# Seven batches of gates transposed by VectorE and DRAM rows, two rows of running sums for the first two slots, and a new list of steps

## The chip, the cores and the metric

The kernel runs on one core of a Trainium2 chip. The metric is the device time of one execution in microseconds (us), lower is better, as the median of several runs. Besides those runs, one execution was profiled; durations are read from that one.

The engines are called PE (TensorE, the matrix unit; PEld is its weight load), DVE (VectorE), ACT (ScalarE), POOL (GpSimd) and SP (SyncE, which here does nothing but issue transfers, in order).

## The reference

The program is a causal attention with a bias from running sums, followed by a mixture of four attention experts of which each token uses two. Cut to what matters:

```python
B, H, S, D = 8, 8, 576, 64
# attention, for each of 64 heads
scores = q @ k.T / sqrt(D)
cum = cumsum(maximum(s, 0))
scores = where(causal, -1e9, scores + minimum(-(cum[:, None] - cum[None, :]), 0))
attn = softmax(scores) @ v
x = heads_side_by_side(attn)                      # 8 batches x 576 x 512
# experts
logits = x @ w_gate                               # 4 per token
topk, w = two_largest(logits), softmax over the two
for e in range(4):
    q, k, v = x @ wq[e], x @ wk[e], x @ wv[e]
    ye = causal_softmax(q @ k.T / sqrt(64)) @ v @ wo[e]
    out += (gate weight of e, zero where not chosen) * ye
```

## The kernel before, in words

**Slots.** The work is a list of 50 slots, numbered 0 to 49, each for a pair of heads: four slots of attention for each of the eight batches, and between them two slots of experts for the batch before. (Slots -2 and -1 only prepare, slot 49 finishes.) A slot's work is cut into small steps, named by a letter and a number. Those that matter here:

- `ld`, `h0` to `h3`, `l0` to `l3`, `lq`, `lk`: loads q and k of a pair (`raw`) and splits them into a leading part (tiles `q_2`, `k_2` and so on, ring `Q2`, `K2`) and a rest (`Q1`, `K1`), for score products that use both.
- `hc`: puts the running sums as extra rows under the keys, from row 64 on, so that the score product adds the bias.
- `m0` to `m5` and `M0` to `M5`: PE multiplies queries and keys into `mx`, DVE takes each row's maximum (line 752) into `mcol`.
- `mt`, `mA`, `mq`: PE transposes the maxima, ACT negates them into `mr` (line 776), SP issues two transfers (line 781) that write them as row 96 of the queries. The score products need that row.
- `s0` to `s6`, `E0` to `E6`: score products on PE, exponentials on ACT into `p`.
- `b`, `d`: POOL masks the diagonal and adds up the columns into `r`. `v0` to `v8`: PE multiplies `p` and `r` by the values (line 914).
- `p0` to `p7`: projections of the experts (line 1144). `g0` to `g3`: the gates of a batch, into tile `gw` (128 x 5 x 4).
- `t0`, `T0`, `t1`, `T1`, `td`: PE transposes `gw` with five small products (line 1256), ACT copies the result to a row tile (line 1263), and one transfer (`gcol<-g`, line 1268) spreads it over the partitions, where it later scales the reciprocals of the expert slots (line 1000).
- `i0` to `i59`: 60 spare products on a tile of zeros (line 1376) that feed no result and keep PE at work in slot -2.

**Order.** The whole order is one written list, `ORDER`, of entries `slot:step`. Each engine executes its own instructions in the order of that list; an instruction waits on semaphores for its operands and for its buffer. All transfers go through the one SP queue, so a transfer that waits holds back all behind it. PE's results go to eight banks that are handed round in the order of the list.

**Slots 0 and 1** (`DIRECT`) don't split their heads: the tile `plain` holds q and k as loaded, and the score products (line 800) run on it in full precision. The running sums of all heads stand in `early`, part of the buffer `PB[1]` (its tile is `p` in the rows), as three rows that add up to the sum: two splits on DVE (`c3`, `c4`; lines 464 and 467) make the leading part, the next part and the rest. `hc` of slots 0 and 1 takes these three rows straight from there, with four transfers (two heads, 512 and 64 columns each; line 631). All other slots take theirs from DRAM (`cum`).

## Time and profile before

| | us |
|---|---|
| median of three runs | 662.95 |
| lowest, highest run | 659.91, 663.21 |
| the profiled execution, its time | 661.08 |
| span of its trace | 659.4 |
| PE busy in the span | 645.2 |
| DVE, ACT, POOL busy | 508.8, 471.6, 414.9 |
| transfers' engines busy, share of the span | 47% |

The span runs from the first to the last instruction of the trace. Busy time of PE counts a product until its modelled end, and products overlap, so the distance between the starts of two neighbours is what a product takes from the line.

### The profile page before, as it was taken

To read this page: it belongs to the slowest core of one execution; us is meant where nothing else is said; L and a number is where in the kernel's file an instruction comes from. 1 tells how busy PE (TensorE), PEld (TensorE's weight loads), DVE (VectorE), ACT (ScalarE), POOL (GpSimd) and SP (SyncE) were. 2 spreads that over 40 slices of the span, in tenths; PEclk is the share of its full clock that TensorE was granted. 3 is DMA by queue.
4 is the path that set the end of the run, shared out by engine and by line. 5 is a ranking of instruction groups with operands and counts; after the bars stand their busy time and mean duration, and the time that the engine had idled before them with its cause. 6 is when DMAs were issued, how large, how long until landed. Compare 5 with 4: busy or idle time off the path is not lost.

```text
span 659.4 us, 16622 instructions
## 1 busy us (share of the span) xinstructions
PE 645.2 (98%) x5921; PEld 531.6 (81%) x5922; DVE 508.8 (77%) x1452; ACT 471.6 (72%) x1091; POOL 414.9 (63%) x557
## 2 busy tenths in 40 slices
PE   7799999999999999999999999999999999999997
PEld 3377698888887898788888888878888888898875
DVE  6488878887888678885789859887788867771884
ACT  3459978877778667787578867687587877576564
POOL 9179756687576665864687639746966668626130
PEclk9799999999999999999999999999999999999999
DMA  6325544533646355564565444636554634320513
GB/s 169 101 91 129 168 134 103 145 93 92 161 114 153 99 127 137 135 187 117 128 163 145 124 115 120 172 104 165 114 161 109 169 68 120 101 88 21 133 40 112
DMA packets 49165, 81.23 MB, mean 123 GB/s; under 512 B 19494, under 2 KB 19494, under 8 KB 49084
## 3 DMA queue, kind: packets, MB, share of 16 engines
q1 hardware_dynamic: 49084, 80.18, 46.3%
q8 instruction: 47, 0.77, 0.5%
q14 instruction: 34, 0.28, 0.1%
HBM read 44.55 MB, written 10.09 MB: 83 GB/s over the span
## 4 chain that ended last, share of the span: by engine, by line
PE 94%; DVE 2%; ACT 1%; DMA 1%; issue 0%; SPq 0%; DVEq 0%; ACTq 0%
PE pvp L914 20%; PE pq L1144 16%; PE s L806 11%; PE s L811 11%; PE mx L738 10%; PE pw L1144 8%; PE po L1144 7%; PE sm L967 4%; PE s L845 1%; PE s L800 1%; PE po L1118 1%; PE mt L772 1%; PE i L1376 1%; DMA q<-mr 1%; PE gt L1256 1%
## 5 line engine op out<-in xcount | busy, mean ns | idle before, releaser
L752 DVE CUSTOM_DVE_ANT_0 sink<-mx,mask 128x64 bf16<-128x64 f32 (+7 forms) x432 | 168.8, 428 | 70.6 <-PE mx L738 56.0
L827 ACT ACTIVATE p<-s 128x512 f32<-128x512 f32 x288 | 160.8, 591 | 44.3 <-PE s L811 32.8
L857 POOL TENSOR_SCALAR_AFFINE_SELECT p<-p 128x256 f32<-128x256 f32 (+1 forms) x192 | 90.8, 481 | 126.5 <-ACT p L827 103.7
L806 PE MATMUL s<-q,k 128*128 128x192 f32 (+2 forms) x552 | 151.9, 299 | 0.0
L811 PE MATMUL s<-q,k 97*128 97x192 f32 (+2 forms) x552 | 141.6, 291 | 0.7 <-DMA q<-mr 0.6
L878 POOL TENSOR_TENSOR r<-r,p 128x640 f32<-128x640 f32 (+1 forms) x92 | 128.6, 1398 | 4.8
L806 PEld LDWEIGHTS s<-q,k 128*128 128x128 f32 x552 | 105.2, 191 | 10.1 <-issue 3.7
L811 PEld LDWEIGHTS s<-q,k 97*128 97x128 f32 x552 | 105.2, 191 | 1.7 <-DMA q<-mr 1.1
L1144 PE MATMUL pq<-x,wqkh 128*128 128x288 f32 x512 | 105.1, 299 | 0.0
L914 PE MATMUL pvp<-p,v 128*64 128x128 f32 (+3 forms) x1024 | 100.6, 322 | 0.0
L713 DVE TENSOR_TENSOR q<-raw,q 64x576 fp32r<-64x576 f32 x92 | 81.7, 905 | 20.1 <-ACT q L678 14.1
L719 DVE TENSOR_TENSOR k<-raw,k 64x1024 fp32r<-64x1024 f32 (+1 forms) x92 | 80.0, 883 | 18.0 <-PE s L806 8.0
L738 PE MATMUL mx<-k,q 96*64 96x256 bf16 (+7 forms) x920 | 87.1, 293 | 0.0
L1144 PEld LDWEIGHTS pq<-x,wqkh 128*128 128x128 f32 x512 | 81.4, 188 | 1.4 <-issue 0.4
L914 PEld LDWEIGHTS pvp<-p,v 128*64 128x64 f32 x1024 | 63.5, 136 | 21.6 <-issue 2.2
L1144 PE MATMUL pq<-x,wqkl 128*128 128x288 f32 x256 | 75.5, 295 | 0.0
L875 POOL TENSOR_TENSOR r<-p 128x384 f32<-128x384 f32 x46 | 47.8, 1038 | 38.6 <-ACT p L827 35.1
L682 ACT ACTIVATE k<-raw 64x128 fp32r<-64x128 f32 (+1 forms) x92 | 61.4, 680 | 10.1 <-DMA raw<-in_qk_dram 5.8
L678 ACT ACTIVATE q<-raw 64x576 fp32r<-64x576 f32 x92 | 61.5, 678 | 4.8 <-DMA raw<-in_qk_dram 3.1
L738 PEld LDWEIGHTS <-q 96*64 96x64 bf16 x920 | 45.9, 110 | 21.5 <-issue 7.5
L857 POOL TENSOR_SCALAR_AFFINE_SELECT r<-p 128x256 f32<-128x256 f32 x48 | 31.5, 655 | 35.4 <-ACT p L827 35.4
L928 ACT ACTIVATE pv<-pvp 128x256 f32<-128x256 f32 (+1 forms) x92 | 36.3, 407 | 23.3 <-PE pvp L914 23.0
(143 smaller groups left out, 1181.6 us busy)
## 6 DMA issues: line engine op xcount, KB each, us to landing
raw<-in_qk_dram SPq DMA_DIRECT2D x30, 576.0 KB
rb<-rr SPq DMA_DIRECT2D x92, 144.0 KB
q<-q SPq DMA_DIRECT2D x45, 288.0 KB
k<-k SPq DMA_DIRECT2D x39, 288.0 KB
v<-in_vm_dram SPq DMA_DIRECT2D x32, 256.0 KB
out_dram<-o SPq DMA_DIRECT2D x32, 256.0 KB
q<-mr SPq DMA_DIRECT2D x92, 2.2 KB
w_qk<-in_wqk_dram SPq DMA_DIRECT2D x4, 256.0 KB
```

What stands on the lines that cost most here:

```text
L678: nc.scalar.activation(q2[0:64, j], get_raw(n)[0:64, j], AF.Copy)
L713: nc.vector.tensor_tensor(a[64:128, j], get_raw(n)[0:64, j], q2[0:64, j].bitcast(F32), op=OP.subtract)
L719: nc.vector.tensor_tensor(part(c[0:64]), get_raw(n)[64:128, :, k], part(c[64:128]).bitcast(F32), op=OP.subtract)
L738: nc.tensor.matmul(t[64 * j : 64 * j + 64, c0 : c0 + k1 - k0], q2[0:RC, 64 * qt : 64 * qt + 64], keys(n)[0:RC, span(j, k0, k1)].bitcast(BF ...
L752: nc.vector.tensor_tensor_reduce(sink[:, c0 : c0 + w], t[:, c0 : c0 + w], mask[:, m0 : m0 + w], scale=1.0, scalar=mcol[n][:, 9:10] if bi = ...
L806: nc.tensor.matmul(t[0:nk, c0 : c0 + q1 - q0], K1[r1(n)][:, span(j, k0, k0 + nk)], Q1[r1(n)][:, j, q0:q1], start=True, stop=False,)
L811: nc.tensor.matmul(t[0:nk, c0 : c0 + q1 - q0], K2[r2(n)][0 : RM + 1, span(j, k0, k0 + nk)], Q2[r2(n)][0 : RM + 1, j, q0:q1], start=False, ...
L827: nc.scalar.activation(ptile[n][:, x % 2, 512 * ci : 512 * ci + 512], tl[x], AF.Exp, scale=0.125)
L857: nc.gpsimd.affine_select(out=a if kt else running()[:, :, 0:128], in_=a, pattern=[[64 if kt == 4 else 0, 2], [1, nk]], compare_op=OP.is_g ...
L878: add(r[:, :, q0:S], r[:, :, q0:S], p[:, :, 1024 + c : 1024 + c + S - q0], op=OP.add)
L914: nc.tensor.matmul(cur[h][64 * j : 64 * j + 64, q0 - PVC[h] : q1 - PVC[h]], vsl(j, kt), rtile[n][:, j, 0:128] if own else ptile[n][:, j, c ...
L1144: nc.tensor.matmul(t[0:nk, 0:w], l, r, start=(x == 0), stop=(x == len(terms) - 1))
```

## The change

Three edits. First, for seven of the eight batches (all but the last) the five PE transposes of `gw` and their two ACT copies go. In their place `tv` is one DVE transpose of a 128 x 32 tile (`gwt`, of which `gw` now is the first 20 columns) in blocks of 32 x 32, `ts` writes its rows to DRAM with four transfers, and `td` reads them back spread over the partitions. Second, slots 0 and 1 take two rows of running sums, leading part and rest, which the first split alone makes; the tail of their scores is two products of 64 x 64, and queries and keys stand in one tile. Third, `ORDER` is new as a whole (3951 entries for 3967).

```diff
 ORDER = (
-    "-2:i37 -2:i18 -2:i23 -2:i7 -2:i21 -2:i39 -2:i12 -2:i31 -2:f12 -2:i9 -2:i30 -2:i22 -2:f20 "
...
+    "-2:i33 -2:i25 -2:i10 -1:z2 -2:z1 -2:i13 -2:i34 0:ld -2:f12 -2:f22 -2:z2 -2:i9 1:h2 -2:i18 "
...
-    gw = const.tile([P, 5, E], F32, tag="gw", name="gw")
+    gwt = const.tile([P, 32], F32, tag="gw", name="gw")
+    gw = gwt[:, 0 : 5 * E].rearrange("p (t e) -> p t e", e=E)
...
-        def split(j):
-            c = t["c"][:n]
+        def cut(x, y):
             nc.vector.tensor_single_scalar(
-                c3[:n, j].bitcast(I32), c.bitcast(I32), -65536, op=OP.bitwise_and
+                y[:n].bitcast(I32), x[:n].bitcast(I32), -65536, op=OP.bitwise_and
             )
-            nc.vector.tensor_tensor(c3[:n, 2] if j else c, c, c3[:n, j], op=OP.subtract)
...
+        def first():
+            cut(t["c"], c4[:, 1])
+            nc.vector.tensor_tensor(c4[:n, 0], t["c"][:n], c4[:n, 1], op=OP.subtract)
+
+        def second():
+            cut(c4[:, 0], c4[:, 2])
+            nc.vector.tensor_tensor(c4[:n, 3], c4[:n, 0], c4[:n, 2], op=OP.subtract)
...
         def sums_in():
             for j in range(2):
                 hd = 2 * i + j
-                for k in (slice(0, 512), slice(512, S)):
-                    nc.sync.dma_start(
-                        keys(n)[64:67, span(j, k.start, k.stop)], early[0][hd : hd + 1, :, k]
-                    )
...
+                nc.sync.dma_start(whole(n)[64:66, 2 + j], early[0][hd : hd + 1, 0:2])
...
             if n in DIRECT:
-                nc.tensor.matmul(
-                    t[:, 0:P], keys(n)[:, 0:P], queries(n)[:, :, q], start=True, stop=True
-                )
+                for j in range(2):
+                    h = slice(64 * j, 64 * j + 64)
+                    nc.tensor.matmul(
+                        t[h, h], keys(n, P, j, 512, S), queries(n)[:, j, q], start=True, stop=True
+                    )
                 return
...
+        def flip():
+            t["w"] = sb.tile([P, 32], F32, tag="gwt", name=f"gwt{b}", bufs=1)
+            nc.vector.transpose(t["w"], gwt)
+
+        def out_rows():
+            t["d"] = dram.tile([E, S], F32, tag="gd", name=f"gd{b}", bufs=2)
+            for x in range(4):
+                m = 5 if x < 2 else 4
+                d = t["d"].rearrange("e (c i) -> c e i", i=32)[x : x + 4 * m - 3 : 4]
+                nc.sync.dma_start(d, t["w"][32 * x : 32 * x + E * m])
+
         def send():
             gcol[b] = sb.tile([P, S // 32], F32, tag="gcol", name=f"gcol{b}", bufs=2)
-            nc.sync.dma_start(gcol[b], t["g4"])
+            nc.sync.dma_start(gcol[b], t["d"].rearrange("e (p c) -> (e p) c", c=S // 32))
...
         if b < B - 1:
-            items["td"] = send
+            items["tv"], items["ts"], items["td"] = flip, out_rows, send
         else:
+            items["t0"], items["T0"] = lambda: turn(0), lambda: copy(0)
+            items["t1"], items["T1"] = lambda: turn(1), lambda: copy(1)
             items["sl"] = select
```

The order of instructions changes in many places; three of them follow. The first is ACT at the start of the program. Before, its first operand to wait for is the sums' input (`s_t`):

```order
L452 ACT_TABLE_LOAD
L452 ACTIVATE s_r<-s_t 64x576
L678 ACTIVATE q_2_70<-raw_155 64x576
L706 ACTIVATE k_0_66<-raw_155 64x1024
L706 ACTIVATE k_0_66<-raw_155 64x128
```

Of the changed kernel, the same place:

```order
L670 ACT_TABLE_LOAD
L670 ACTIVATE q_0_68<-raw_120 64x576
L452 ACTIVATE s_r<-s_t 64x576
L670 ACTIVATE q_0_68<-raw_120 64x576
L698 ACTIVATE k_1_67<-raw_120 64x1024
```

A copy from a pair's loaded heads (`raw_120`, here those of slot 3) now stands ahead of the sums' input. In the SP queue that pair's load moved to the front as well. Before, the queue opens so (`p_94` is the buffer with the running sums):

```order
L448 DMA s_t<-in_s_dram 64x576
L563 DMA raw_155<-in_qk_dram 128x2x576
L643 DMA plain<-in_qk_dram 64x2x576
L495 DMA w_qk_177<-in_wqk_dram 128x512
L637 DMA plain<-in_qk_dram 64x2x64
L637 DMA plain<-in_qk_dram 64x2x512 x2
L631 DMA plain<-p_94 3x1x512
L631 DMA plain<-p_94 3x1x64
```

And in the changed kernel:

```order
L566 DMA raw_120<-in_qk_dram 128x2x576
L448 DMA s_t<-in_s_dram 64x576
L636 DMA plain<-in_qk_dram 64x2x576
L635 DMA plain<-in_qk_dram 64x2x576 x2
L566 DMA raw_215<-in_qk_dram 128x2x576
L632 DMA plain<-p_94 2x1x576 x2
L636 DMA plain<-in_qk_dram 64x2x576
L632 DMA plain<-p_94 2x1x576 x2
```

Two transfers instead of four bring the sums of a slot, and a second pair's load stands ahead of them. The second place is PE after the maxima of slot 0 (`mt_289`, `mt_330` are the transposes of slot 0's maxima, `i` spare products, `s_4` and so on the score chunks of slot 0). Before, with the rows between left out:

```order
L738 MATMUL mx_3_282<-plain 64x512
L772 MATMUL mt_289<-ident,mcol_251 9x128
L738 LDWEIGHTS plain
L738 MATMUL mx_3_301<-plain 64x512
...
L1376 MATMUL i_306<-sink 128x512
...
L738 MATMUL mx_5_335<-plain 64x256
...
L1376 MATMUL i_387<-sink 128x512
L800 MATMUL s_4_389<-plain 128x320
L800 MATMUL s_4_389<-plain 128x192
L1376 LDWEIGHTS sink
L1376 MATMUL i_392<-sink 128x512
```

Of the changed kernel:

```order
L730 MATMUL mx_4_326<-plain 64x512
L764 MATMUL mt_330<-ident,mcol_282 9x128
L1381 LDWEIGHTS sink
L1381 MATMUL i_332<-sink 128x512
...
L1381 MATMUL i_389<-sink 128x512
L792 MATMUL s_5_392<-plain 128x320
L792 MATMUL s_5_392<-plain 128x192
L792 MATMUL s_4_397<-plain 128x320
L792 MATMUL s_4_397<-plain 128x192
L792 MATMUL s_0_403<-plain 128x256
L792 MATMUL s_0_403<-plain 128x256
```

All six `mx` banks of slot 1 moved ahead of `mt`, the spare products after `mt` stand in one run of 20 (before, 11 and then 9 more among products of slots 0 and 1), and the six score chunks follow each other with none between. The third place is the gates of the first batch. PE before:

```order
L806 MATMUL s_2_1891<-q_1_65,k_1_67 128x192
L811 MATMUL s_2_1891<-q_0_68,k_0_71 128x192
L1256 MATMUL gt_0_1901<-ident,gw 4x128 x4
L806 MATMUL s_3_1909<-q_1_65,k_1_67 128x320
L811 MATMUL s_3_1909<-q_0_68,k_0_71 128x320
L806 MATMUL s_3_1909<-q_1_65,k_1_67 128x192
L811 MATMUL s_3_1909<-q_0_68,k_0_71 128x192
L1256 MATMUL gt_512_1921<-ident,gw 4x64
L806 MATMUL s_1_1923<-q_1_65,k_1_67 128x256
```

In the changed kernel PE has no such products there, and the SP queue has four transfers more (`gd` are the rows in DRAM):

```order
L773 DMA q_1_69<-mr_1947 1x9x64 x2
L663 DMA k_0_71<-cum 3x1152
L693 DMA q_1_65<-q_2_70 64x1152
L1269 DMA gd_2017<-gwt_1794 5x4x32 x2
L1269 DMA gd_2017<-gwt_1794 4x4x32 x2
L700 DMA k_1_67<-k_2_73 64x1152
...
L989 DMA sr_2335<-rs_2168 128x1x18
L1273 DMA gcol_2347<-gd_2017 128x18
```

Over the whole list, PE goes from one of two kinds of product to the other (those that fill a part of the array's columns, `mx`, `pvp` and `sm`, and those that fill all) 139 times before and 127 times now.

## Rows read from the trace of the kernel before

**Rows 1.** The page, part 1: busy us (share) x instructions of each engine.

```profile
PE 645.2 (98%) x5921; PEld 531.6 (81%) x5922; DVE 508.8 (77%) x1452; ACT 471.6 (72%) x1091; POOL 414.9 (63%) x557
```

**Rows 2.** Busy time by stretch; columns as in its first line.

```profile
core 0: us, PE busy (x) PEld busy (x) DVE busy (x) ACT busy (x) POOL busy (x), PEclk, DMA share, GB/s
...
14.00:17.70 3.70, 0.28 (x4) 0.00 (x0) 3.49 (x19) 0.31 (x1) 3.57 (x4) 1.00 0.68 216
17.70:24.60 6.90, 5.09 (x13) 1.71 (x14) 2.44 (x4) 2.21 (x5) 1.63 (x2) 0.51 0.77 207
...
36.30:131.00 94.70, 94.47 (x906) 75.85 (x905) 78.67 (x238) 78.12 (x173) 69.74 (x96) 1.00 0.49 132
...
655.30:659.40 4.10, 0.03 (x1) 0.00 (x0) 0.00 (x0) 0.59 (x1) 0.00 (x0) 1.00 0.37 117
```

**Rows 3.** Timeline of PE, 0 to 40 us: start, us, line, operation [wait <- releaser].

```profile
1.35 10.15 PE L1376 MATMUL i<-sink 128*128 128x512 bf16 x40 [1.35 <-DVE sink L375]
...
12.69 1.60 PE L738 MATMUL mx<-plain 96*64 96x448 bf16 x19 [0.88 <-DMA plain<-p]
17.77 0.37 PE L772 MATMUL mt<-ident,mcol 128*9 128x128 f32 x1 [3.49 <-DVE mcol L752]
...
21.92 2.99 PE L1376 MATMUL i<-sink 128*128 128x512 bf16 x7 [0.22 <-PE i L1376]
...
32.74 3.72 PE L800 MATMUL s<-plain 128*128 128x320 f32 x16 [1.67 <-ACT p L827]
36.30 0.27 PE L772 MATMUL mt<-ident,mcol 128*9 128x128 f32 x1
```

**Rows 4.** Timeline of the SP queue, 0 to 45 us: the transfers that it issues.

```profile
9.19 2.98 SPq L631 DMA_DIRECT2D plain<-p  x4
...
18.47 1.55 SPq L781 DMA_DIRECT2D plain<-mr  x2
```

**Rows 5.** Timeline of ACT, 0 to 38 us.

```profile
3.64 0.68 ACT L452 ACTIVATE s_r<-s_t 64x576 f32<-64x576 f32 x1 [1.55 <-DMA s_t<-in_s_dram]
6.51 0.69 ACT L678 ACTIVATE q<-raw 64x576 fp32r<-64x576 f32 x1 [2.19 <-DMA raw<-in_qk_dram]
```

**Rows 6.** Timeline of DVE, 0 to 18 us.

```profile
5.16 1.35 DVE L457 TENSOR_TENSOR_SCAN s_c<-s_r 64x576 f32<-64x576 f32 x1
6.54 0.47 DVE L464 TENSOR_SCALAR p<-s_c 64x576 int32<-64x576 int32 x1
7.04 0.75 DVE L467 TENSOR_TENSOR s_c<-s_c,p 64x576 f32<-64x576 f32 x1
...
16.87 0.75 DVE L752 CUSTOM_DVE_ANT_0 sink<-mx,mask,mcol 128x512 bf16<-128x512 f32 x1
```

**Rows 7.** Timeline of PE, 130 to 133 us, in the first batch of gates.

```profile
131.40 0.27 PE L811 MATMUL s<-q,k 97*128 97x192 f32 x1
131.51 0.60 PE L1256 MATMUL gt<-ident,gw 128*4 128x128 f32 x4
131.87 0.39 PE L806 MATMUL s<-q,k 128*128 128x320 f32 x1
...
132.34 0.28 PE L811 MATMUL s<-q,k 97*128 97x192 f32 x1
132.54 0.21 PE L1256 MATMUL gt<-ident,gw 64*4 64x64 f32 x1
132.69 0.39 PE L806 MATMUL s<-q,k 128*128 128x256 f32 x1
```

**Rows 8.** Timeline of the SP queue, 620 to 627 us.

```profile
622.66 1.55 SPq L781 DMA_DIRECT2D q<-mr  x2
```

**Rows 9.** Timeline of PE, 626 to 627.5 us.

```profile
627.09 0.41 PE L811 MATMUL s<-q,k 97*128 97x320 f32 x1 [0.59 <-DMA q<-mr]
```

**Rows 10.** Timeline of the SP queue, 128 to 175 us.

```profile
138.42 0.64 SPq L1268 DMA_DIRECT2D gcol<-g  x1
```

**Rows 11.** Timeline of DVE, 128 to 160 us.

```profile
158.51 0.33 DVE L1000 TENSOR_TENSOR sr<-sr,gcol 128x18 f32<-128x18 f32 x1
```

More of the change, by code (lines that the diff above doesn't have):

```diff
@@ L427, in late_constants @@
                 nc.gpsimd.memset(PB[i][64 - 64 * j : 128 - 64 * j, j, PT:PCOLS], 0.0)
+        nc.gpsimd.memset(gwt, 0.0)
         nc.gpsimd.memset(tlt, 0.0)
@@ L476, in keep_sums @@
             for k in (slice(0, 512), slice(512, S)):
-                nc.sync.dma_start(cum[:, :, span(j, k.start, k.stop)], early[0][j : B * H : 2, :, k])
+                nc.sync.dma_start(cum[:, :, span(j, k.start, k.stop)], early[0][j : B * H : 2, 1:4, k])
     def weights(name):
@@ L605, in whole, with keys @@
     def whole(n):
-        if n not in plain and n < 2:
-            w = sb.tile([P, 2, 2, 2, S], F32, tag="x", name="plain", bufs=1)
-            for m in range(2):
-                plain[m] = w[:, m, 0], w[:, m, 1].rearrange("p j s -> p (j s)")
-        elif n not in plain:
-            q, k = (sb.tile([P, 2, S], F32, tag="raw", name=f"plain{n}{x}", bufs=3) for x in "qk")
-            plain[n] = q, k.rearrange("p j s -> p (j s)")
+        if n not in plain:
+            w = sb.tile([P, 2, 4, S], F32, tag="x", name="plain", bufs=1)
+            for x, m in enumerate(DIRECT):
+                plain[m] = w[:, x]
         return plain[n]
     def queries(n):
-        return whole(n)[0] if n in DIRECT else Q2[r2(n)]
-    def keys(n):
-        return whole(n)[1] if n in DIRECT else K2[r2(n)]
+        return whole(n)[:, 0:2] if n in DIRECT else Q2[r2(n)]
+    def keys(n, rows, j, k0, k1):
+        if n in DIRECT:
+            return whole(n)[0:rows, 2 + j, k0:k1]
+        return K2[r2(n)][0:rows, span(j, k0, k1)]
     def direct(n):
@@ L740, in bank @@
                         q2[0:RC, 64 * qt : 64 * qt + 64],
-                        keys(n)[0:RC, span(j, k0, k1)].bitcast(BF16)[:, 1::2],
+                        keys(n, RC, j, k0, k1).bitcast(BF16)[:, 1::2],
                         start=True, stop=True,
@@ L801, in seg @@
                     t[0:nk, c0 : c0 + q1 - q0],
-                    keys(n)[:, span(j, k0, k0 + nk)], queries(n)[:, j, q0:q1],
+                    keys(n, P, j, k0, k0 + nk), queries(n)[:, j, q0:q1],
                     start=True, stop=True,
```

31 lines of the change are left out of this document (11 added, 20 removed), and 512 rows, old and new, of the table ORDER.

## The prediction

> **What bounds the kernel now.** I read the page's busy times first, then busy time by stretch, then PE's timeline where a stretch isn't full, and last the places that the change touches. PE is busy 645.2 of the span's 659.4 us, the next engine, DVE, 508.8 [rows 1]. From 36.3 to 131 us PE works 94.47 of 94.70 us [rows 2], and the stretches up to 655.3 look the same: the one wait of weight in them is 0.59 us, for a transfer of maxima [rows 9]. So after the start a microsecond less on PE is a microsecond less in the end, and what DVE, ACT, POOL or SP do counts only where PE comes to wait for it. The end is a fixed tail: PE does 0.03 us after 655.3, then come a last copy and store, 4.1 us [rows 2]. The start is what isn't full. PE runs 40 spare products from 1.35 us on, gets slot 0's last sums at 12.69, stops until 17.77 for DVE to finish the row maxima, and comes to slot 1's transposed maxima, the next `mt`, at 36.30 [rows 3]. From there on PE is full, so the time at which that `mt` is reached is the yardstick for the start.
>
> **Gates.** Four transposes start at 131.51, the next product at 131.87: 0.36 us. The fifth takes from 132.54 to 132.69, 0.15 us, and the product ahead of it holds the line 0.20 us (132.34 to 132.54) where the same product ahead of the four takes 0.11: 0.09 more [rows 7]. That is 0.60 us a batch, seven batches 4.2 us. Without the 0.09 it is 3.6; with it twice, 4.8. The row's own 0.60 us for four is the overlapped time and would overprice them. The Trainium skill (TensorE: Matmul & The Clock Gate, Part 4: PE-mode transpose) gives about 275 ns for such a transpose in a kernel; by that, 35 of them would be an estimated 9.6 us. The trace agrees only for one transpose taken alone and not for a row of them, so the spacing decides: **-4.2**.
>
> What comes in for them lies elsewhere. A DVE transpose of 128 x 32 isn't in the trace; the nearest row is a DVE product of 18 columns, 0.33 us [rows 11], against 0.75 for 576 columns [rows 6]: 0.2 to 0.75 us, on an engine that is idle 23% of the span, while ACT loses 14 copies. The 28 additional transfers are at 0.64 us of SP each [rows 10] 18 us in all, 2.6 a batch. Their result is due late: the old `gcol` transfer is issued at 138.42 and first used at 158.51 [rows 10, 11], 20 us later, so a second trip through DRAM, a few us, has cover. What the four can delay is what stands behind them in SP: above all `mq`, for which the scores wait. I price this at 0 and keep it as a rival.
>
> **The sums of slots 0 and 1.** Before, two splits of 0.47 + 0.75 us (with their gaps 1.3 each) precede the transfers of the sums, issued from 9.19 us on [rows 4, 6]; the third of four, 1.5 us after the first, is the one that PE gets at 12.69 [rows 3], so about 2.0 us from issue to use. Now one split goes ahead: -1.3. But the new list puts a copy of a pair's heads ahead of the sums' input on ACT. Before, ACT started the sums at 3.64 and had a pair's heads only at 6.51 [rows 5]; that load now goes first in SP, ahead of the one that stood before it (0.67 us), so heads arrive at about 5.8, the copy takes 0.69, and the sums start at 6.5, end at 7.2; the scan (1.35) ends at 8.6, the split at 9.9. The second of two transfers is issued 0.75 us later, 10.6, and used at 12.6 or, if the pair's load ahead of it holds it up, 1.5 us later. So the two rows bring slot 0's maxima forward by **0**: what the second split gave, the new order spends.
>
> **The start after that.** The last maximum of slot 0 begins at 16.87 and `mt` follows at 17.77 [rows 6, 3]. In the new list PE does all of slot 1's maxima in that pause, ahead of slot 0's last bank, for whose sums it has to wait; I allow 0.4 us and put `mt` at 18.2. `mr` and SP's two issues before took from 17.77 to 18.47 + 1.55 = 20.02 [rows 3, 4], 2.25 us; so the issues end at 20.4. How long they take to land I take from a case where PE waits: issued until 624.21, used at 627.09, 2.9 us [rows 8, 9], so 23.3; where transfers meet less, 1.5 us earlier. Meanwhile PE runs 20 spare products. At the half clock one takes 2.99 / 7 = 0.427 us [rows 3], granted 0.51 of full in that stretch [rows 2]; at the full one half of it, 0.21. From 18.6 on that is until 22.8 or 27.1. At the full clock the scores begin at 23.3. Four chunks take 32.74 to 36.30, 0.89 each [rows 3]; six take 5.3, so the next `mt` is reached at 28.6. The tail chunk of slot 0, done by then before, isn't yet: at most one half-chunk, 0.3 us. DVE must have slot 1's maxima by then: after 18.2 it has five subtractions and a memset, near 0.75 us each, some 4.7 us, then slot 1's ten reductions, which for slot 0 took from 12.69, when PE got the sums, to 17.62, 4.9 at most [rows 3, 6]: 27.8, just in time. So PE is ahead by 36.30 - 28.6 - 0.3 = **-7.4**. Why so much: before, 11 of the spare products ran at the half clock, slot 1's maxima came after `mt` instead of in the pause, and score chunks waited 1.67 us for an exponential [rows 3] behind copies on ACT.
>
> **The rest of the list.** PE changes between the two kinds of product 12 times less. The nearest price is the 0.09 of rows 7, to which a change of kind should be alike, so **-1.1**; it may be 0, and 12 times 0.2 is 2.4. The end of the list has the same parts in another order: 0, give or take 1.5. The 64 x 64 tails are two slots' worth of 0.3 us: 0.
>
> **Sum.** -4.2 - 7.4 - 1.1 = -12.7 against the profiled execution's 661.1 (span 659.4 and 1.7 around it): 648.4. The median of the runs lies 1.9 above that execution; beside it the forecast is 650.2. I say **650**, for itself 645 to 654.
>
> **Rivals.** (1) The spare products run at half clock. Before, the granted clock fell after a stretch in which PE worked 0.28 of 3.7 us and came back only after spares had run without a break [rows 2, 3]. If the new pause, with slot 1's maxima in it, is still too empty, the scores start at 27.1, `mt` comes at 32.4, and the start gives 3.6: sum -8.9, **654**. The Trainium skill (TensorE: Matmul & The Clock Gate, Part 1) has the slow state as the default that activity must release; this trace agrees with 0.51 of the clock in that stretch. (2) SP gives part back: in two of seven batches `mq` stands close behind the new transfers. Two to five us in all: **655**. (3) The start isn't shorter, because the heads of two pairs, loaded first, hold up sums and maxima by 7 us: by the shapes in the order the bytes asked for ahead of slot 0's sums grow from 1.85 to 2.21 MB; against it, transfers keep up with 0.68 of their engines busy from 14 to 17.7 [rows 2]. Then gates and list alone remain, -5.3: **658**. (4) Slower: each of the seven blocks of four pushes an `mq`, and with it PE, by its whole 2.6 us and more through the transfer behind it: from 1.8 us a batch the whole gain of 12.7 is gone, and at 2.6, 18 us, the kernel takes **668**. Against it: PE waited for `mq` only once, 0.59 us [rows 9], so there is room at most places.
>
> **How the numbers follow.** Forecast 0.52, rival 1 0.20, rival 2 0.12, rival 3 0.09, rival 4 0.07. A measurement of this kernel tells some 0.5%, 3.3 us, from no change; faster means below 659.6. Forecast, rivals 1 and 2 and most of 3 lie there; leaving some of each for what the new list may do in the middle: faster 0.85, same 0.09, slower 0.06. The range takes the bounds of gates and tail below (644) and reaches to rival 3 above (658).
>
> **What would show it.** Right: no line of gate transposes but for the last batch (5 of 40 left); slot 0's sums used by PE at 12 to 14 us, no earlier than before; slot 1's `mt` at 28 to 30; full PE from there to 4 us before the end; spares after slot 0's `mt` some 0.21 us apart. Wrong: spares at 0.43 apart (rival 1), new waits of PE for `mr` behind the `gd` transfers (2, 4), first scores after 28 us (3), or a stall in the middle that no row here foretells.

## The result, and the profile after

The changed kernel takes 652.18 us (median of four runs, 650.63 to 653.66) against 662.74 for the kernel before in the same measurement: ratio 0.9849, 95% interval 0.9813 to 0.9886, so 7.6 to 12.4 us faster. The profiled execution is the longest of the four, 653.66 us with a span of 651.9; before it was 661.08 with 659.4. The forecast was 650, with a range of 644 to 658, and the reasons held only in part: the gates gave what was forecast, the start gave 1.0 us of 7.4, and what hid that in the median stands in the section on the prediction.

The page of the kernel after, part 1 (for the kernel before: [rows 1]):

```profile
PE 639.9 (98%) x5891; PEld 529.3 (81%) x5891; DVE 514.0 (79%) x1459; ACT 467.4 (72%) x1077; POOL 414.4 (64%) x558
```

The timeline of PE in the kernel after, beside [rows 3]:

```profile
12.60 0.36 PE L730 MATMUL mx<-plain 96*64 96x448 bf16 x1 [0.53 <-DVE p L473]
13.25 1.23 PE L730 MATMUL mx<-plain 96*64 96x448 bf16 x17 [0.29 <-DMA plain<-p]
16.33 3.04 PE L730 MATMUL mx<-plain 96*64 96x256 bf16 x22 [1.86 <-DMA w_qk<-in_wqk_dram]
20.32 0.37 PE L764 MATMUL mt<-ident,mcol 128*9 128x128 f32 x1 [0.94 <-DVE mcol L744]
20.48 9.52 PE L1381 MATMUL i<-sink 128*128 128x512 bf16 x20
29.89 5.60 PE L792 MATMUL s<-plain 128*128 128x320 f32 x24
35.33 0.27 PE L764 MATMUL mt<-ident,mcol 128*9 128x128 f32 x1
```

Busy time by stretch in the same kernel, beside [rows 2] (columns: stretch, length, busy time and count of instructions of PE, PEld, DVE, ACT and POOL, granted clock of PE, share of the transfer engines, GB/s):

```profile
5.50:15.00 9.50, 8.15 (x49) 3.76 (x47) 7.06 (x12) 5.86 (x10) 8.83 (x24) 1.00 0.75 171
15.00:16.00 1.00, 0.00 (x0) 0.00 (x0) 1.00 (x9) 0.99 (x2) 1.00 (x2) 0.75 0.59 194
16.00:20.00 4.00, 3.04 (x22) 1.65 (x22) 1.83 (x9) 0.93 (x2) 3.84 (x5) 0.50 0.83 233
20.50:25.00 4.50, 4.11 (x8) 0.76 (x7) 4.10 (x6) 2.46 (x4) 0.00 (x0) 0.50 0.10 26
25.00:28.90 3.90, 3.89 (x10) 1.38 (x10) 0.32 (x1) 0.00 (x0) 0.00 (x0) 0.50 0.77 236
29.20:35.00 5.80, 5.80 (x26) 4.09 (x25) 4.28 (x20) 3.06 (x6) 1.39 (x4) 1.00 0.07 18
```

Slot 0's `mt` stands at 20.32 (17.77 before), the first score at 29.89, slot 1's `mt` at 35.33: 0.97 us ahead of before, where the prediction put 7.4. The clock is at its lower level (1.2 GHz, 0.50) from the middle of 15 to 16 us on until shortly before the scores, most of the time between the first maxima and them. In the stretch from 20.5 to 25 us, PE gets through 8 products (`mt` and seven spares), from 25 to 28.9, at the same clock, through ten spares.

ACT's timeline in the start, beside [rows 5]:

```profile
5.94 0.68 ACT L670 ACTIVATE q<-raw 64x576 fp32r<-64x576 f32 x1 [3.84 <-DMA raw<-in_qk_dram]
6.60 0.68 ACT L452 ACTIVATE s_r<-s_t 64x576 f32<-64x576 f32 x1
```

DVE's, beside [rows 6]:

```profile
7.32 1.35 DVE L457 TENSOR_TENSOR_SCAN s_c<-s_r 64x576 f32<-64x576 f32 x1 [2.21 <-ACT s_r L452]
8.70 1.05 DVE L463 TENSOR_SCALAR p<-s_c 64x576 int32<-64x576 int32 x1
...
19.41 0.75 DVE L744 CUSTOM_DVE_ANT_0 sink<-mx,mask,mcol 128x512 bf16<-128x512 f32 x1 [2.02 <-PE mx L730]
...
30.04 0.63 DVE L744 CUSTOM_DVE_ANT_0 sink<-mx,mask 128x448 bf16<-128x448 f32 x1 [4.72 <-PE i L1381]
```

The new steps of the gates over the whole span (minimum, median, maximum in ns, first and last start):

```profile
L1269 SPq DMA_DIRECT2D gd<-gwt x28: 599/668/1322, 135.0 to 591.2; - x28
L1262 DVE STREAM_TRANSPOSE gwt<-gw x7: 196/211/213, 123.5 to 588.7; 128x32 f32<-128x32 f32 x7
```

Two waits on DVE stand out. Slot 0's last maximum waits 2.02 us for PE, because its bank (`m4`) is listed behind slot 1's maxima, which wait for their heads and sums until 16.33 and then run at half clock (3.04 us). Slot 1's first maximum waits 4.72 us for `i`, a spare product: the spares read `sink`, and `sink` is also the tile into which DVE writes the throw-away output of its reductions.

PE's waits of 0.9 us and more behind its first product (line, tile, releaser, total, times, longest):

```profile
PE mx L730 <- DMA w_qk<-in_wqk_dram: 1.9, 1, 1.9
...
PE s L803 <- DMA q<-mr: 1.3, 1, 1.3
PE mx L730 <- ACT p L844: 1.0, 1, 1.0
PE mt L764 <- DVE mcol L744: 0.9, 1, 0.9
```

The `q<-mr` wait stands behind the product that starts at 56.67, the `ACT p` wait behind the one at 448.63; the kernel before had one of 0.59 [rows 9]. For the sum of PE's work, the time from each product's start to the next one's, by the tile that is written, over the whole span (count, us; `all` has the tiles not shown in it, too):

```
         before          after           old_gates       gates_alone
gt         48   6.59      13   2.82       48   7.55       13   2.83
i          59  18.99      60  20.66       60  19.15       59  19.42
mx, mt   1008  78.40    1008  75.58     1008  75.46     1008  78.03
s        1248 171.31    1252 169.25     1252 169.75     1248 175.98
pvp      1728 136.00    1728 135.26     1728 135.83     1728 138.29
pq        768 104.84     768 105.73      768 107.78      768 105.59
all           653.60         646.23          652.49          657.88
```

Here a wait is counted with the product ahead of it. `gt` holds the gate transposes: 3.77 us less after. Of the 7.4 us between the two profiled executions this is half.

### The profile page after: what moved, and what is told of

Its sections match the earlier page's. It is cut to its first block, busy times and chain, and to the rows that moved or that the text cites. A ratio compares the mean times of both kernels' runs of the same rounds, so it can differ in the third digit from the quotient of the medians.

```text
span 651.9 us, 16521 instructions
## 1 busy us (share of the span) xinstructions
PE 639.9 (98%) x5891; PEld 529.3 (81%) x5891; DVE 514.0 (79%) x1459; ACT 467.4 (72%) x1077; POOL 414.4 (64%) x558
## 4 chain that ended last, share of the span: by engine, by line
PE 92%; DMA 3%; ACT 2%; DVE 1%; SPq 1%; issue 1%; ACTq 0%; DVEq 0%
PE pvp L908 20%; PE pq L1138 16%; PE s L798 11%; PE s L803 10%; PE mx L730 10%; PE pw L1138 9%; PE po L1138 7%; PE sm L961 4%; DMA raw<-in_qk_dram 2%; PE s L792 2%; PE i L1381 1%; PE s L839 1%; PE po L1112 1%; PE mt L764 1%; ACT p L819 1%
## 5 line engine op out<-in xcount | busy, mean ns | idle before, releaser
L851 POOL TENSOR_SCALAR_AFFINE_SELECT p<-p 128x256 f32<-128x256 f32 (+1 forms) x192 | 95.4, 506 | 142.0 <-ACT p L819 117.0
L798 PE MATMUL s<-q,k 128*128 128x320 f32 (+2 forms) x552 | 149.7, 297 | 0.0
L803 PE MATMUL s<-q,k 97*128 97x320 f32 (+2 forms) x552 | 141.4, 290 | 1.3 <-DMA q<-mr 1.3
L705 DVE TENSOR_TENSOR q<-raw,q 64x576 fp32r<-64x576 f32 x92 | 78.7, 870 | 25.2 <-ACT q L670 9.0
L711 DVE TENSOR_TENSOR k<-raw,k 64x1024 fp32r<-64x1024 f32 (+1 forms) x92 | 82.7, 913 | 13.7 <-PE s L798 6.0
L730 PE MATMUL mx<-k,q 96*64 96x512 bf16 (+7 forms) x920 | 86.3, 293 | 1.0 <-ACT p L844 1.0
L908 PEld LDWEIGHTS pvp<-p,v 128*64 128x64 f32 x1024 | 63.7, 136 | 23.3 <-issue 3.0
L730 PEld LDWEIGHTS <-q 96*64 96x64 bf16 x920 | 45.0, 110 | 19.7 <-issue 6.2
L867 POOL TENSOR_TENSOR r<-p 128x256 f32<-128x256 f32 x46 | 37.4, 812 | 34.1 <-ACT p L819 34.1
L869 POOL TENSOR_TENSOR r<-p 128x384 f32<-128x384 f32 x46 | 49.2, 1070 | 11.3 <-ACT p L819 11.2
```

The lines of the kernel that those rows point to most:

```text
L705: nc.vector.tensor_tensor(a[64:128, j], get_raw(n)[0:64, j], q2[0:64, j].bitcast(F32), op=OP.subtract)
L711: nc.vector.tensor_tensor(part(c[0:64]), get_raw(n)[64:128, :, k], part(c[64:128]).bitcast(F32), op=OP.subtract)
L730: nc.tensor.matmul(t[64 * j : 64 * j + 64, c0 : c0 + k1 - k0], q2[0:RC, 64 * qt : 64 * qt + 64], keys(n, RC, j, k0, k1).bitcast(BF16)[:, 1 ...
L798: nc.tensor.matmul(t[0:nk, c0 : c0 + q1 - q0], K1[r1(n)][:, span(j, k0, k0 + nk)], Q1[r1(n)][:, j, q0:q1], start=True, stop=False,)
L803: nc.tensor.matmul(t[0:nk, c0 : c0 + q1 - q0], K2[r2(n)][0 : RM + 1, span(j, k0, k0 + nk)], Q2[r2(n)][0 : RM + 1, j, q0:q1], start=False, ...
L851: nc.gpsimd.affine_select(out=a if kt else running()[:, :, 0:128], in_=a, pattern=[[64 if kt == 4 else 0, 2], [1, nk]], compare_op=OP.is_g ...
```

## The experiments

Each kernel was timed in up to five rounds beside the kernel before. `slot 0 mt`, `score` and `slot 1 mt` are starts on PE in the profiled execution, read from its timeline: slot 0's transposed maxima, the first score product, slot 1's transposed maxima.

| kernel | median us | ratio to before, 95% | slot 0 mt | score | slot 1 mt |
|---|---|---|---|---|---|
| before | 662 to 663 | 1 | 17.77 | | 36.30 |
| predicted for the change | 650 | | 18.2 | 23.3 | 28.6 |
| after | 652.18 | 0.9813 to 0.9886 | 20.32 | 29.89 | 35.33 |
| ten_in_pause | 650.89 | 0.9815 to 0.9871 | 22.35 | 28.36 | 33.79 |
| no_second_spares | 648.89 | 0.9781 to 0.9839 | 18.04 | 21.49 | 29.72 |
| ten_early | 659.72 | 0.9945 to 0.9982 | 20.31 | 32.86 | 40.81 |
| m4_first | 649.37 | 0.9771 to 0.9829 | 18.43 | 26.63 | 32.07 |
| own_chain | 649.51 | 0.9791 to 0.9840 | 19.34 | 26.35 | 31.71 |
| m4_chain8 | 648.04 | 0.9764 to 0.9809 | 18.43 | 21.98 | 28.06 |
| mt_first | 647.02 | 0.9752 to 0.9800 | 18.43 | 21.89 | 28.06 |
| sums_ahead | 644.66 | 0.9699 to 0.9756 | 17.62 | 21.27 | 27.52 |
| old_gates | 661.29 | 0.9964 to 1.0000 | 20.41 | 28.46 | 33.90 |
| old_gates_late | 665.90 | 1.0034 to 1.0078 | | | |
| gates_alone | 666.11 | 1.0038 to 1.0084 | | | |
| ts_behind_mq | 664.01 | 1.0018 to 1.0051 | | | |

The marks are of one execution each. Up to slot 0's `mt` the lists of after, old_gates, own_chain and no_second_spares are the same, and yet it starts at 20.32, 20.41, 19.34 and 18.04; after and old_gates share the list up to slot 1's `mt`, too, which starts at 35.33 and 33.90 (the clock is back at 29.1 and at 26.2). So a difference of one or two us in a mark can be the execution's. By the intervals, m4_chain8, mt_first and sums_ahead are clear of the changed kernel; ten_in_pause, no_second_spares, m4_first and own_chain overlap with it, so that their medians alone don't show them faster.

The theory going in: gates are worth their 4 us on PE, and the start fell short because the 20 spares behind `mt` ran at half clock. The rivals: the transfers of the gates cost what PE gains, and the start is bounded by something else (the transfer of maxima, or DVE).

### The gates, from both sides

**old_gates.** The new list, with the old gates.

```diff
-        if b < B - 1:
-            items["tv"], items["ts"], items["td"] = flip, out_rows, send
-        else:
-            items["t0"], items["T0"] = lambda: turn(0), lambda: copy(0)
-            items["t1"], items["T1"] = lambda: turn(1), lambda: copy(1)
+        items["t0"], items["T0"] = lambda: turn(0), lambda: copy(0)
+        items["t1"], items["T1"] = lambda: turn(1), lambda: copy(1)
+        if b < B - 1:
+            items["td"] = send
 ORDER, seven times: the entry tv goes, and ts and td give way, at the place of ts, to
+ 9:t0 (six entries) 9:T0 9:t1 (six entries) 9:T1 9:td
```

> The changed kernel with the gates of all batches transposed on TensorE again (35 transposes and 14 copies on ACT back, the DVE transposes and the 28 transfers gone), the rest as changed. By the gate term of the prediction this costs 4.2 us (3.6 to 4.8): 656.4 us. Rival 1: the new transfers on SP cost PE as much as the transposes did (the wait for q<-mr at 56.67 us comes from them), then 652 or less. Rival 2: a transpose costs about 0.28 us wherever it stands, then 35 of them give 661 to 662 us.

Measured 661.29 us, 9.1 more than the changed kernel. The table of PE's work above has the transposes at 4.73 more (with 1.0 of waits among them), so the direct term stands near 3.7; more waits come with these places in the list: PE's for `gw` (1.3 us, counted in `pq` with the product ahead of it, where it is most of the 2 us more) and for `p` (0.7, 0.6). The profiled executions, 651.9 and 658.1 us in span, are only 6.2 apart, so the rows account for 6.2 of the 9.1. That the transfers cost as much as the transposes (rival 1) is out for this list. The total is that of rival 2, but not by its reason: thirty-five transposes with their waits come to 0.135 us each, and stand 0.11 apart in a row of four. The Trainium skill (TensorE: Matmul & The Clock Gate, Part 4: PE-mode transpose) gives about 275 ns in a kernel, for a transpose of 128 x 128 in bf16. The smaller ones here last 214 to 276 ns each, near that figure, but overlap; what PE's line pays is the measured spacing, half of it, and that decides.

**old_gates_late.** As old_gates, with `t0` to `td` of two batches 40 places later.

> As old_gates (all batches transposed on TensorE again), with the transposes of two batches 40 places later in the list, where DVE has long finished the gates; in old_gates PE waited 1.3 us for gw and ACT's copies held up others. Theory: of the 9.1 us that old_gates lost, some 4 are such waits, and 5 are the transposes themselves with the products around them: 658 to 659 us. Rival: the waits come back elsewhere, the list has no room for the old gates: 661.

Measured 665.90: worse, so the theory's 658 to 659 fell and the rival understated it. SP's queue in old_gates_late at the dearest place:

```profile
297.28 0.27 SPq L665 DMA_DIRECT2D k<-cum  x1
303.21 0.67 SPq L1275 DMA_DIRECT2D gcol<-g  x1
303.93 1.54 SPq L775 DMA_DIRECT2D q<-mr  x2
```

PE's timeline there:

```profile
303.50 0.42 PE L800 MATMUL s<-q,k 128*128 128x320 f32 x1
306.56 0.64 PE L805 MATMUL s<-q,k 97*128 97x320 f32 x1 [2.64 <-DMA q<-mr]
```

And the stretch behind it (columns as for the kernel after):

```profile
307.00:312.00 5.00, 5.00 (x23) 5.00 (x22) 3.51 (x12) 0.60 (x1) 0.00 (x0) 0.50 0.76 182
```

SP holds `gcol<-g` until ACT has copied the late transposes, from 297.6 to 303.21, and the maxima `q<-mr` stand behind it; PE waits 2.64 us. Then it works 5 us without a pause at half clock, which costs an estimated 2.5 us more (half of 5.00 us busy at 0.50).

**gates_alone.** The old list and start, with the new gates: `tv` at the place of the first transpose, `ts` at most 50 entries behind it, `td` at the old place or up to 60 entries behind `ts`.

```diff
-            items["td"] = send
+            items["tv"], items["ts"], items["td"] = flip, out_rows, send
 ORDER, for the first batch
- 9:t0 ... 9:t1 ... 9:T1 ... 9:T0 ... 9:td
+ 9:tv ... 9:ts ... 9:mt ... 9:mq ... 9:td
```

> The kernel before with the new gates alone: DVE transposes, four transfers to DRAM and one back for seven batches, put where the old steps stood; list, sums and start of before. By the gate term: 4.2 us less than before, 658.5 us. Rival: in a list that was not laid out for them the 28 transfers hold up the transfers of maxima, and PE waits for q<-mr in several batches: 662 us or more.

Measured 666.11, 0.6% slower than before, although the same 3.8 us of `gt` are gone. SP's queue in gates_alone, in the first batch:

```profile
131.67 2.85 SPq L1276 DMA_DIRECT2D gd<-gwt  x4
134.56 0.54 SPq L709 DMA_DIRECT2D k<-k  x1
135.21 3.36 SPq L1010 DMA_DIRECT2D rb<-rr  x4
138.67 1.60 SPq L782 DMA_DIRECT2D q<-mr  x2
```

PE's timeline:

```profile
141.26 0.41 PE L812 MATMUL s<-q,k 97*128 97x320 f32 x1 [2.99 <-DMA q<-mr]
```

The stretch behind it:

```profile
143.00:146.00 3.00, 3.00 (x32) 2.56 (x28) 3.00 (x7) 2.64 (x6) 2.84 (x3) 0.50 0.51 106
```

Four issues of `gd` take 2.85 us, `q<-mr` goes out that much later (138.67; before, 135.60), and PE waits 2.99 us for it. Two other waits for `q<-mr`, 0.65 and 0.71 us, make it 4.4 in all. So rival 4 of the prediction, put there at 0.07, came in kind in a list that was not laid out for the new gates: at three places and not with all seven batches, with a total (666.1) near its 668.

**ts_behind_mq.** In four batches `ts` behind the next `mq`.

```diff
- 9:ts ... 9:mt ... 9:v3 9:mq
+ 9:mt ... 9:v3 9:mq 9:ts
```

> The kernel before with the new gates alone, as gates_alone, but in four batches (slots 9, 21, 33, 39) the four transfers of the gates stand behind the next transfers of maxima in SP's queue, not ahead of them. Theory: gates_alone lost because the gates' transfers (2.85 us of SP) held up the transfers of maxima (q<-mr waits of 3.0 us and less, mt behind them, the clock after them). Then the waits of PE for q<-mr go, and the gates' own gain shows: 658 to 660 us against 666.1. Rival: DVE's and DRAM's part of the new gates costs it, or the clock: 664 or more.

Measured 664.01: two us better, not the six that the theory wanted. The waits of PE for `q<-mr` shrink from 4.4 to 1.8 us, but near 303 us the four issues (292.68 to 295.5) now stand ahead of a transfer of keys. DVE's timeline in ts_behind_mq:

```profile
305.02 0.29 DVE L720 TENSOR_TENSOR k<-raw,k 64x128 fp32r<-64x128 f32 x1 [5.17 <-DMA k<-k]
```

DVE waits 5.17 us for it, a slot's maxima and with them its `mt` come late, PE waits 2.83 us, and the granted clock is 0.50 from 307 to 310. Before, `k<-k` went out from 294.20 to 295.73 and landed at 300.04; here it goes out from 298.42 to 298.92 and lands at 305.0, with the transfer engines 0.84 to 0.99 busy from 298 on. So the four issues make it some three us late, and what the fuller transfer engines add was not told apart. The cost of the four transfers is at least in part a place in SP's queue, and moving them hands it to the next in line.

**The two halves together.** Against the kernel before, the new list and sums without the new gates take 0.2% less (old_gates, 0.9982), the new gates without the new list 0.6% more (gates_alone, 1.0061), both together 1.5% less. Neither half explains the gain alone, so a share of it for each, as in the sums below, is read from the rows of one execution and holds for this pair only.

### The start

**no_second_spares.** The 20 spares behind `mt` are left out of the list.

```diff
-SPARE = 60
+SPARE = 40
 ORDER
- -2:i40 ... -2:i59
```

> The changed kernel without the 20 spare products after slot 0's mt. Theory (the spares at half clock hold the scores back, the maxima have landed at 25.5 us): the first score begins at 25.5 and not 29.9. But nothing then brings the clock up before the scores, so they run at half clock for some us, and of 4.4 us won 1 to 3 are lost again: 649 to 651 us. Rival 1: the spares earn more than they cost, the scores all run at half clock: 653 to 656. Rival 2: the maxima land only near 29 us, scores begin there: 652 or more.

Measured 648.89, at the edge of the theory's 649 to 651. The timeline of PE in no_second_spares:

```profile
18.04 0.27 PE L763 MATMUL mt<-ident,mcol 128*9 128x128 f32 x1 [0.94 <-DVE mcol L743]
21.49 8.40 PE L791 MATMUL s<-plain 128*128 128x320 f32 x24 [3.18 <-DMA plain<-mr]
```

`mt` stands at 18.04 because in this execution the clock stayed full until 20.5; the list ahead of `mt` is that of the kernel after. The first score comes at 21.49, 3.45 us after `mt`: that is how long the maxima travel, so in the changed kernel they should have landed by some 23.8, and the spares held the scores back for six us. The 24 score products take 8.2 us here against 5.4 in the kernel after: they start at half clock. Leaving the 20 spares out is as good as mending them in own_chain below (649.51; the intervals overlap).

**ten_in_pause.** Ten more spares between slot 0's maxima and slot 1's.

```diff
-SPARE = 60
+SPARE = 70
- 0:m5
+ -2:i60 ... -2:i69 0:m5
```

> The changed kernel with ten additional spare products in the pause of PE between slot 0's first maxima and slot 1's (14.5 to 16.3 us); the 20 after slot 0's mt stay. Theory: the start gave little because the clock fell in that pause. Then the granted clock stays full, the 20 spares take 4.3 us and not 9.5, the scores begin when the maxima have landed, near 25.5 us and not 29.9, and slot 1's mt comes at 31 and not 35.3: 648 us. Rival 1: ten more products only lengthen the start, 2.1 us more at full or 4.3 at half clock, if the clock falls all the same: 652 to 656. Rival 2: the transfer of maxima or DVE sets the time of the scores, and nothing changes: 652.

Measured 650.89; against 652.18 no clear difference. It tests the theory badly: the ten started only at 16.10, after a wait of 1.7 us for DVE, whose reductions ahead of them in the list write `sink`, which they read. The next expectation blames a bank for it; that was wrong, since the first of the ten takes a free one. In this execution the clock was back at 18.8, ahead of `mt`, and the 20 spares behind it still took 5.9 us: the first seven 0.43 apart, the others 0.22. So something besides half clock spaced the first seven.

**ten_early.** The same ten ahead of DVE's first reductions; the 20 spares behind `mt` become one row, all ahead of `mA`.

```diff
-SPARE = 60
+SPARE = 70
- -2:M0
+ -2:i40 ... -2:i49 -2:M0
 ORDER, behind -1:mt
- -2:i40 ... -2:i59
+ -2:i50 ... -2:i69
```

> The changed kernel with ten additional spare products, listed right behind slot 0's first five maxima and ahead of DVE's reductions, so that they take banks that nobody holds (in the run with ten in the pause the spares waited until 16.10 us for a bank, and the clock had fallen at 15.42). Theory: PE works through the pause, the clock stays full, slot 1's maxima take 1.7 us, the 20 spares after mt 4.3 us, the scores begin near 24 us and slot 1's mt comes near 29.5 instead of 35.3: 646 to 647 us. Rival 1: the clock falls all the same near 15.5 us, the ten add 2 to 4 us: 652 to 655. Rival 2: DVE has slot 1's maxima only near 33 us, and what the scores win is lost before its mt: 650.

Measured 659.72: all three guesses were too good. The timeline of PE in ten_early:

```profile
13.39 2.33 PE L1382 MATMUL i<-sink 128*128 128x512 bf16 x10
15.65 0.79 PE L731 MATMUL mx<-plain 96*64 96x256 bf16 x8
...
20.31 0.27 PE L765 MATMUL mt<-ident,mcol 128*9 128x128 f32 x1 [1.31 <-DVE mcol L745]
20.41 12.34 PE L1382 MATMUL i<-sink 128*128 128x512 bf16 x20
32.86 8.12 PE L793 MATMUL s<-plain 128*128 128x320 f32 x24
```

And the spares behind `mt` by stretch (columns as for the kernel after):

```profile
22.00:32.00 10.00, 9.16 (x16) 1.61 (x16) 2.94 (x5) 1.10 (x2) 0.00 (x0) 0.50 0.38 116
```

The ten ran at once and at full clock, 0.22 apart. But DVE then had to wait for them, since they read `sink`: its reductions began at 15.88 and not 13.79, and `mt` came no earlier than in the kernel after. And the 20 behind `mt` take 12.34 us, nearly all of them 0.64 apart, though the half clock alone gives 0.43. At that place of the list the banks are given out but for one (six hold slot 1's maxima, one `mt`), so all 20 write that one, and the spacing says that each waits until the one before it has ended (0.64 at half clock, as for the first seven of the kernel after; 0.43 at full clock, as for the first seven of ten_in_pause). In the kernel after it is one bank for the first seven and two, in turn, for the other 13; in the kernel before, seven banks went round.

**m4_first.**

```diff
- 0:m5 0:m3 0:m4 -1:m0 -1:m1 ... -1:m2 -1:M5 -1:M3 -1:m4 -1:M4 -1:mt
+ -1:m4 0:m5 0:m3 0:m4 -1:m0 -1:m1 ... -1:M5 -1:M3 -1:m2 -1:M4 -1:mt
```

> The changed kernel with slot 0's last bank of maxima (m4) ahead of slot 1's maxima, and slot 1's m2 behind DVE's last reductions but one. Theory: the last reduction of slot 0 waited 2.0 us for that bank; without this wait mt comes at 18.3 and not 20.3 us, the spares still run at half clock, scores at 27.9: 650 us. Rival: mt is earlier but the clock, with PE idle longer before it, stays low for longer, and nothing is won: 652 to 653.

Measured 649.37 (runs from 645.02 to 651.02). The timeline of PE in m4_first:

```profile
18.43 0.37 PE L765 MATMUL mt<-ident,mcol 128*9 128x128 f32 x1 [0.47 <-DVE mcol L745]
```

`mt` is at 18.43, as expected; the scores begin at 26.63, with the first spares still 0.64 apart, the next 0.43, and those behind 24.5, where the clock is back, 0.22. DVE's first maximum of slot 1 waits 3.34 us for a spare here too.

**own_chain.** The 20 spares where they are, as one accumulation, reading zeros that nobody writes: two changes at once.

```diff
 def spare(x):
-    t = take(f"i{x}")
-    nc.tensor.matmul(t, sink[:, 0:P], sink, start=True, stop=True)
-    give(t)
+    # a, z: first and one behind the last of the chain (40, 60)
+    if x == a:
+        held[a] = take(f"i{x}")
+    t = held[a]
+    r = sink if x < 40 else mask[:, 0:512]
+    nc.tensor.matmul(t, r[:, 0:P], r, start=x == a, stop=x == z - 1)
+    if x == z - 1:
+        give(t)
```

> The changed kernel with its 20 spare products after slot 0's mt in the same place, but written as one accumulation in one bank (no product waits for the end of the one before) and reading the mask's zeros instead of the scratch tile that DVE's reductions write. In the changed kernel the first seven stood 0.64 us apart (0.583 of one product and a wait for it, one bank), and DVE's first reduction of slot 1 waited 4.7 us for the last spare. Theory: 0.43 apart from 20.5 us on, so the clock is back earlier, spares end near 26 and not 29.9, slot 1's mt near 31.5: 648 to 649 us. Rival 1: the spacing comes from the clock or from the fetching of instructions, and stays 0.64: 652. Rival 2: DVE, freed earlier, has nothing to win, and the spares' gain is lost at slot 1's mt: 651 to 652.

Measured 649.51, the theory's number a little exceeded. The spares of the kernel after, first seven (minimum, median, maximum in ns; first and last start):

```profile
L1381 PE MATMUL i<-sink x7: 583/583/631, 20.5 to 24.4; 128*128 128x512 bf16 x7
```

The spares of own_chain up to the clock's return:

```profile
L1389 PE MATMUL i<-mask x12: 588/631/631, 19.5 to 24.2; 128*128 128x512 bf16 x12
```

From the first start to the last it is 0.64 us a spare there (its own 0.583 and the next one's start behind it) and 0.43 here. The clock is back at 24.6 and not shortly after 28.9; that the chain brought it back is not shown, since it is back at 24.5 in m4_first and at 26.2 in old_gates, where the spares are serial. Slot 1's `mt` comes 3.6 us earlier; 1.0 of these is slot 0's `mt`, as the maxima ahead of it ran partly at full clock in this execution. The spacing goes with the accumulation (spares that read `sink`, too, stood 0.427 apart in the kernel before, over several banks), DVE's wait with the operand; what each is worth was not told apart. The Trainium skill (Perfetto Trace Analysis, Optimizing Tensor Performance, Matmuls) advises that independent groups of products rotate through the banks so that one can be emptied while the next is worked on, and says that an accumulation group keeps to one bank. Nobody empties the spares' bank, so that reason is not the one here; this trace shows 0.64 us for groups in one bank and 0.43 for a chain in one, at the same clock.

**m4_chain8** and **mt_first.** With the chain of own_chain: the first is m4_first with 8 spares behind `mt`; the second has all of slot 0's maxima and `mt` ahead of slot 1's maxima, 16 spares ahead of `mt`, 6 behind slot 1's maxima.

```diff
 mt_first, ORDER
- -2:M0 -2:M1 -2:M2 -2:f01 0:m5 ... -1:m2 -1:M5 -1:M3 -1:m4 -1:M4 -1:mt -2:i58 ...
+ -1:m4 -2:i40 ... -2:i55 -2:M0 -2:M1 -2:M2 -2:f01 -1:M5 -1:M3 -1:M4 -1:mt -1:mA 0:m5 ... -1:m2 -2:i56 ... -2:i61
```

> As m4_first (slot 0's last bank of maxima ahead of slot 1's), with 8 instead of 20 spare products after mt, in one bank and reading the mask. Theory: mt at 18.4, the maxima have landed 3.4 us later (18.04 to 21.49 in the run without second spares), the 8 fill that wait at half clock, the scores begin at 22 us, the clock comes back among them and not at 27.3, slot 1's mt at 28.5: 645 to 646 us. Rival: the scores run at half clock as they did without spares, mt at 29.7 or later: 647 to 649.

> The changed kernel with slot 0's last bank, reductions and mt ahead of slot 1's maxima; 16 spare products in one bank, reading the mask, in the pause of PE ahead of mt, and 6 behind slot 1's maxima. Theory: PE never pauses for 1 us, the clock stays full, mt at 18.4, slot 1's maxima in the 3.4 us while slot 0's maxima travel, scores from 22 us at full clock, 5.5 us, slot 1's mt at 27.5 to 28: 643 to 645 us. Rival 1: DVE has slot 1's reductions only near 30 us: 646 to 647. Rival 2: the clock falls all the same: 649 or more.

Measured 648.04 and 647.02: in both the start is where the theories put it, slot 1's `mt` at 28.06, and the time is 2 us above them. In the middle of both stand waits that the theories did not have: in m4_chain8 one of 1.07 us at 256 and a stretch at half clock from 621.7 to 625.0, in mt_first one of 1.03 us at 356.6. The timeline of PE in mt_first:

```profile
12.82 1.87 PE L732 MATMUL mx<-plain 96*64 96x448 bf16 x20
14.62 3.63 PE L1389 MATMUL i<-mask 128*128 128x512 bf16 x16
18.43 0.27 PE L766 MATMUL mt<-ident,mcol 128*9 128x128 f32 x1 [0.18 <-DVE mcol L746]
18.63 1.48 PE L732 MATMUL mx<-plain 96*64 96x256 bf16 x20
20.04 1.47 PE L1389 MATMUL i<-mask 128*128 128x512 bf16 x6
21.89 5.60 PE L794 MATMUL s<-plain 128*128 128x320 f32 x24 [0.38 <-DMA plain<-mr]
28.06 0.28 PE L766 MATMUL mt<-ident,mcol 128*9 128x128 f32 x1 [0.56 <-DVE mcol L746]
```

Two of its stretches (columns as for the kernel after):

```profile
16.00:20.00 4.00, 3.82 (x32) 1.72 (x30) 3.65 (x12) 1.29 (x4) 3.84 (x5) 1.00 0.82 231
20.50:25.00 4.50, 4.12 (x19) 2.77 (x18) 4.13 (x13) 2.71 (x6) 0.37 (x2) 1.00 0.48 142
```

PE has no pause of a microsecond, the granted clock is 1.00 in every stretch, and slot 1's `mt` waits 0.56 us for DVE. This is the prediction's start with its conditions met: 28.06 against 28.6. Between this kernel and the changed one the start differs by 7.3 us, the spans by 6.5, the medians by 5.2. It is not the work of one execution: the mean granted clock is 0.988 to 0.991 in all four executions of the changed kernel, 0.997 to 1.000 in all six of mt_first and 0.999 to 1.000 in all five of sums_ahead.

**sums_ahead.** As mt_first, with the sums' input first on SP and ACT and 33 spares at the very start.

```diff
- -2:i33 ... -1:z0 -2:i26 -2:c0 -2:c1 -2:c2
+ -2:c0 -2:c1 ... -1:z0 ... -2:c2
```

> As mt_first, with the sums' input and their activation ahead of the first pair's heads on SP and ACT (as in the kernel before) and 33 instead of 40 spare products at the very start. Theory: the prediction put it that the new order spends what one split gave, and mt_first shows ACT taking up the sums at 6.30 us, behind a copy that waits 3.6 us for its load. Then the sums start near 3.7, DVE's scan ends at 5.8, PE uses slot 0's sums at 10.5 to 11 and not 12.8, mt at 16.4, slot 1's mt at 26: 645 us. Rival 1: slot 0's or slot 1's heads or DVE's other work then come last (heads of slot 1 land near 16 us), and 0 to 1 us is left: 646 to 647. Rival 2: a pause opens in PE, the clock falls, 649 or more.

Measured 644.66, the fastest of all: 2.7% below the kernel before. The sums were issued at 8.23 and not 10.64, but PE could start only at 12.34, when slot 0's heads had landed (rival 1), and slot 1's `mt` gained 0.5. The profiled executions, 645.4 and 641.1 us in span, differ by 4.3, the medians by 2.4. The 3.8 us behind the start are mostly waits in the middle that this execution lacks: mt_first has one of 1.03 us at 356.62, others near 0.3 at 316, 442 and 622, and smaller ones; behind the start no wait of PE in sums_ahead reaches 0.25. Such waits (the one at 56.67 in the kernel after is another) come and go with a shift of the start, in lists that are the same from there on; why, stays open.

## Why the prediction was right, and where not

**Gates, -4.2.** Right, within its bounds of 3.6 and 4.8: 3.77 in `gt`, five of 40 transposes left, and a DVE transpose takes 0.21 us, the lower end of 0.2 to 0.75. The 28 issues take 0.67 us of SP each (0.64 predicted), and no wait of PE is put down to them in this list; sums_ahead has the same 28 and no wait of 0.25 us behind the start. That "cover" is the list's doing, as gates_alone shows: the price of zero held for this order only.

**Sums, 0.** Right on the way, and a little off at the end: ACT takes the sums up at 6.60 (6.5 predicted), the scan ends at 8.67 (8.6), the cut took 1.05 us and not 0.47. The 12.69 that the prediction started from is the last sums; their products start at 13.25, so they came 0.6 later than before and not 0. (12.60 is the first head.)

**The start, -7.4.** Wrong: 1.0 on its own yardstick. The failed step is "At the full clock the scores begin at 23.3"; they begin at 29.89, and three things stood in the way. (a) `mt` at 20.32 and not 18.2: slot 0's last bank stands behind slot 1's maxima, which the prediction saw, and allowed 0.4 us for, and DVE waits 2.02 for it. About half of that is the place in the list (own_chain 19.34, m4_first 18.43, with the clock falling at nearly the same time: 0.9), the other half that slot 1's maxima ran at half clock (3.04 us; 1.97 in own_chain). (b) The clock fell at 15.5, before the spares began, as rival 1 feared, and was back at 29.1. (c) The first seven spares were 0.64 apart, for a third reason, one bank. All three are gone in mt_first, and there the step holds: slot 1's `mt` at 28.06 for the 28.6 predicted. That the spares kept DVE from `sink` for 4.72 us cost nothing here, as slot 1's `mt` follows the scores without a wait; with earlier scores it would have.

So rival 1 was the better forecast of the start and was itself too kind: it had scores at 27.1. Of the signs of being wrong three came: spares at 0.43 and more apart; first scores after 28, which the prediction tied to rival 3, whose reason did not hold (the sums were 0.6 us late and not 7); and a wait of 1.3 us for maxima behind 56.67, though ahead of the first `gd` (135.0) and so not by rivals 2 and 4. The terms around the failed step were near or off in the good direction: six chunks take 5.4 us (5.3 predicted), and the maxima travel from `mt` to the scores in 3.45 us and not in 5.1 (23.3 - 18.2). The 2.9 us from the last issue to the use, taken from [rows 8, 9], is 1.2 here (20.28 to 21.49 in no_second_spares): of the ten landing marks of that transfer in the trace before, nine stand by 625.22, the last at 627.05.

**The rest, -1.1.** Too small: of the 7.4 us between the profiled executions 3.8 are gates and 1.0 the start, so 2.6 came from the rest, net of some 2 us of new waits. Part of it is start that the yardstick misses: most of what the table shows for `mx, mt` lies ahead of slot 1's `mt`, and by products done, the gates' left out, some 1.5 of the 2.6 were won between slot 1's `mt` and the first gates. For the changes of kind there is a price in the rows: a product ahead of one stands 0.15 us longer than one ahead of its own kind (behind 40 us, waits left out), 132 places and 19.7 us before, 119 places and 18.5 after. That is 1.2, as the term of -1.1 said. The other 1.4, and the entries of the list that gave it, stay open.

**The forecast.** 648.4 was the sum for the profiled execution, which took 653.66: 5.3 too low, from a start that was 6.4 us too good, a rest that was 1.5 too small and gates 0.4 too good. The median came as near as 2.2 to 650 because the execution profiled before lies 1.9 below its median and the one profiled after 1.5 above its own, as the slowest of the four. These 3.4 us are luck; rival 1's 654 stood as near, at 1.8.
